# Two attention blocks on one core: zero-weight matmuls in TensorE's gaps, and first scores on 256 tokens

## The chip, the cores and the metric

The kernel runs on one core of a Trainium2 chip. The metric is the device time of one execution in microseconds, the median of several runs. The engines are TensorE (PE; its weight loads are listed apart as PEld), ScalarE (ACT), VectorE (DVE), GpSimd (POOL), and SyncE (SP), which only issues transfers here. Each runs its own list of instructions in order and waits on semaphores for the others.

## The reference, cut to what matters

Two attention blocks, A and B, on 2048 tokens of width 1024 with 32 heads of width 32, all in bf16. Their outputs stand side by side. A is full attention. B works on four segments of 512 tokens, with causal attention in a segment and a memory M, z of all segments before it.

```python
# A
qkv = x @ wqkv; q, k, v = heads of it
p = softmax(q k^T * 32**-0.5); a = (p v) @ wo
# B: for segment s of 4
logits = qs ks^T * scale + causal mask
a_dot = softmax(logits) @ vs
phi = lambda t: where(t > 0, t + 1, exp(t))
a_mem = (phi(qs) @ M) / (phi(qs) @ z + 1e-6)
o = g * a_mem + (1 - g) * a_dot            # g = sigmoid(beta), per head
M = M + phi(ks)^T @ vs;  z = z + sum of phi(ks)
b = o @ wo
return concatenate([a, b], -1)
```

## The kernel before

The order of instructions on each engine is made by a small event-driven scheduler in the Python program that builds the kernel. Each piece of work is a process that asks for an engine, with what it reads and writes, an assumed cost and a priority. The scheduler plays all engines with these costs and so fixes each engine's list; semaphore waits follow from what is read and written. At run time nothing is reordered.

The work comes in units. A unit of A is one group of four heads and 256 queries; it has eight batches, each of 256 keys. A batch is eight score matmuls (`s_batch`), two exponentials of 128x1024 on ScalarE (`exps`), which read PSUM and write PT, and later sixteen matmuls (`pv_unit`) that take PT times V and PT times ones, for output and denominator. Three pairs of PSUM banks hold scores; two further banks (`side`) serve all else.

```python
PAIRS = [(0, 1), (2, 3), (4, 5)]
OB, SB = 6, 7
RING = 27                                  # PT buffers of 512; slots are pairs, RING // 2
par = dict(b=(12, 7, 2), mem=4, ..., ahead=28, ..., ob=2, ..., wob=40, ...)

# s_batch: needs K of 512 tokens and Q of 512 tokens
yield ("ev", ("KA", g, k // 2))
yield ("ev", ("QA", g, u[2] // 2))
...
# exps
yield do("ACT", lambda e: e.activation(ap, self.ps[:, pr[0]:pr[1] + 1, :], ACTF.Exp, scale=sc), ...)   # L900
```

A projection (`proj`, `job`) takes 512 tokens: eight steps of four matmuls side by side, then a copy out of PSUM on VectorE.

```python
def job(self, due, mm, keys, out, okey, wkeys, ...):
    bank, = yield acq(self.side, 1, due)
    for i in range(n):
        yield do("PE", lambda e, i=i: mm(e, i, bank), ..., cost=N512, ...)                             # L610
    op = yield do(eng, lambda e: out(e, bank, eng), r=[("ps", bank)] + ..., cost=c, prio=1)            # L616, L617
```

The start loads the first four tiles of x (128 tokens each), transposes them on TensorE and copies them to xA, in turn on VectorE and ScalarE. Matmuls on zeros (`warm`) stand between. The other 1536 tokens come by transposing DMA. After a `yield do` of a transfer the process goes on when the transfer is issued, so an event such as `("XS", 2)` orders issues and is no wait for data.

```python
# first_x
banks = yield acq(self.pairs, 3)
for t in range(4):
    Q.spawn(self.load_xs(t, "SP" if t % 2 == 0 else "ACT"))          # L570
yield self.warm(8)                                                    # L532
for t in range(4):
    ...                                    # eight transpositions of 128x128, L550
    yield self.warm((4, 4, 4, 8)[t])
    if t % 2 == 0:                         # DVE tensor_copy, L557
    else:                                  # ACT copy, L559
...
Q.give(self.pairs, list(PAIRS))
# rest_x: six transposing DMAs of 256 tokens, L579
# first_w: weights of K (SP) and Q (ACT) after the four x tiles, of V later, L480
# a_prep order: K 0, Q 0, K 1, V 0, K 2, V 1, ...
```

The end of a unit copies the whole bank, output and denominator, in one piece; phi of B is computed on VectorE, since `po=(1, 1)` chooses this branch always.

```python
# finish
yield do("DVE", lambda e: e.tensor_copy(OD[:, :], self.ps[:, OB, :]), ...)                             # L1028
# b_mem: phi (L719 to L731), then the memory's matmuls (L746, L774) with
due = self.first[("B", n)] + self.par["mem"]
# b_proj: before block n, waits for ("fin", "B", n-2) and ("memB", n-2)
# out_B: eight output rows of a segment, each due par["ob"] after the one before                       # L1075
```

Of the kernel before, what the change touches and what calls it, by code (L numbers as in the profile page):

```python
# [9 lines left out]
ALU = mybir.AluOpType  # L10
# [3 lines left out]
P = 128  # L14
# [157 lines left out]
class Sched:  # L172
# [3 lines left out]
    def __init__(self, rec):  # L176
        self.R = rec
        self.now = 0.0
        self.heap = []
        self.seq = 0  # L180
        self.q = {e: [] for e in Recorder.ENG}
        self.free = {e: 0.0 for e in Recorder.ENG}
        self.wake = {e: None for e in Recorder.ENG}
        self.busy = {e: 0.0 for e in Recorder.ENG}
        self.mode = None
        self.dma_free = 0.0
        self.margin = {}
        self.hold = {}
        self.events = {}
        self.log = []  # L190
        self.nproc = 0

# [85 lines left out]
    def dispatch(self, eng, t):  # L278
        if self.wake[eng] != t:
            return  # L280
        self.wake[eng] = None
        if self.free[eng] > self.now + 1e-9:
            self.kick(eng)
            return
        best, soon = None, None
        for rq in self.q[eng]:
            ready = 0.0
            for d in self.R.deps("SP" if rq.kb else eng, rq.r, rq.w, rq.order):
                if d.eng != eng and d.end + LAT > ready:
                    lat = LAT  # L290
                    if rq.prio != 0 or eng != "PE":
                        lat += self.margin.get((eng, d.eng[0]), 0.0)
                    ready = max(ready, d.end + lat)
                elif d.eng == eng and d.end + (LAT if rq.order else 0) > ready:
                    ready = d.end + (LAT if rq.order else 0)
            p = rq.prio() if callable(rq.prio) else rq.prio
            if p > 0 and self.hold.get(eng, 0.0) > ready:
                ready = self.hold[eng]
            if ready <= self.now + 1e-9:
                if best is None or (p, rq.seq) < best[0]:  # L300
                    best = ((p, rq.seq), rq)
            elif soon is None or ready < soon:
                soon = ready
        if best is None:
            if soon is not None:
                self.wake[eng] = soon
                self.at(soon, lambda: self.dispatch(eng, soon))
            return
        rq = best[1]
        self.q[eng].remove(rq)  # L310
        assert all(k in self.R.lastw for k in rq.r), rq.r
        op = self.R.add("SP" if rq.kb else eng, rq.fn, rq.r, rq.w, rq.order, eng)
        cost = rq.cost
        if eng == "PE":
            if rq.mode != self.mode:
                cost += 0.1
                self.mode = rq.mode
        start = self.now
        self.free[eng] = start + cost
        op.end = start + cost + rq.tail  # L320
        if rq.kb:
            self.dma_free = max(self.dma_free, start + min(cost, 0.6)) + rq.kb / 230
            op.end = max(start + cost, self.dma_free) + 1.7
        self.busy[eng] += cost
        self.hold[eng] = start + cost + rq.hold if rq.hold else 0.0
        self.log.append((eng, start, cost, rq.mode))
        if rq.proc is not None:
            self.step(rq.proc, op)
        self.kick(eng)
# [31 lines left out]
RING = 27  # L361
# [4 lines left out]
class Kernel:  # L366
    par = dict(b=(12, 7, 2), mem=4, memM=2, span=50, rate=0.58, ahead=28, sl=4, pv=24, ob=2, lead=5, b0=1, bpos=16, wob=40, mg=0.05, off=0, oks=(1, 4), sh=2, pd=4, o0=4, od=8, run=6, po=(1, 1), fp=2)
# [48 lines left out]
    def alloc(self):  # L416
# [39 lines left out]
        self.ones32 = sb("ones32", [P, 32])  # L456
        self.maskbd = sb("maskbd", [P, P], F32)
# [53 lines left out]
    def constants(self):  # L511
# [5 lines left out]
        yield pool(lambda e: e.memset(self.ones32[:, :], 1.0), ["ones32"])  # L517
        for i in range(2):
            yield pool(lambda e, i=i: e.memset(self.VB[i][:, :, :], 1.0), [("VB", i)])
# [15 lines left out]

    def first_x(self):
        Q = self.Q
        banks = yield acq(self.pairs, 3)
        banks = [b for pr in banks for b in pr]
        for t in range(4):  # L540
            Q.spawn(self.load_xs(t, "SP" if t % 2 == 0 else "ACT"))
        yield do("DVE", lambda e: e.memset(self.PT[:, 0, :], 0.0), w=[("PT", 0)], cost=0.3, prio=0)
        yield self.warm(8)
        for t in range(4):
            yield ("ev", ("XS", t))
            b = banks[t]

            def f(e, t=t, b=b):
                for i in range(NI):
                    ins = e.transpose(self.psb[:, b, P * i:P * i + P], self.XS[:, t, P * i:P * i + P], self.ident[:, :])  # L550
                return ins
            yield do("PE", f, r=[("XS", t), "ident"], w=[("ps", b)], cost=0.9, prio=0, mode=FULL)
            yield self.warm((4, 4, 4, 8)[t])
            src = self.psb[:, b, :].rearrange("p (i n) -> p i n", i=NI)
            dst = self.xA[:, :, P * t:P * t + P]
            if t % 2 == 0:
                Q.spawn(self.one(do("DVE", lambda e, s=src, d=dst: e.tensor_copy(d, s), r=[("ps", b)], w=[("xA", 0, t)], cost=0.6, prio=0), t))  # L557
            else:
                Q.spawn(self.one(do("ACT", lambda e, s=src, d=dst: e.copy(d, s), r=[("ps", b)], w=[("xA", 0, t)], cost=1.0, prio=0), t))  # L559
        for t in range(4):  # L560
            yield ("ev", ("x0t", t))
        Q.fire(("xA", 0))
        Q.give(self.pairs, list(PAIRS))
# [9 lines left out]
    def rest_x(self):  # L573
        yield ("ev", ("WA", 1, 0))
# [9 lines left out]
    def job(self, due, mm, keys, out, okey, wkeys, scale=None, eng="DVE", cost=None, okeys=(), gate=None):  # L584
# [3 lines left out]
        n = len(keys)  # L588
        for i in range(n):
            if gate and gate[0] == i:  # L590
                yield ("ev", gate[1])
            yield do("PE", lambda e, i=i: mm(e, i, bank), r=keys[i] + list(wkeys), w=[("ps", bank)], cost=N512,
                     prio=(lambda: self.jprio(due)) if i == 0 else (lambda: min(self.jprio(due), self.par["run"])), mode=COL)
        if eng == "any":
            eng = "ACT" if (self.s_done and Q.free["ACT"] < Q.free["DVE"]) else "DVE"
        c = dve(512) if eng == "DVE" else 0.6
# [10 lines left out]
    def proj(self, due, W, wkey, x, xkeys, dst, dkey, scale=None):  # L607
        def mm(e, i, bank):
            for c in range(4):
                ins = e.matmul(self.ps[32 * c:32 * c + 32, bank, :], W[:, i, 32 * c:32 * c + 32], x(i),  # L610
# [3 lines left out]
        def out(e, bank, eng):  # L614
            if scale is None:
                return e.tensor_copy(dst, self.ps[:, bank, :])  # L616
            return e.tensor_scalar(dst, self.ps[:, bank, :], scale, None, ALU.mult)  # L617
        return (yield from self.job(due, mm, [xkeys] * NI, out, [dkey], [wkey]))
# [5 lines left out]
    def a_prep(self, g):  # L624
# [6 lines left out]
        xk = lambda c: [("xA", c, t) for t in range(4)]  # L631
        x = lambda c: (lambda i: self.xA[:, i, 512 * c:512 * c + 512])
# [8 lines left out]
        order += [("Q", 1), ("Q", 2), ("Q", 3)]  # L641
        kind = {"K": 0, "Q": 1, "V": 2}
        for w, c in order:
            k = kind[w]
            yield ("ev", ("WA", k, g))
            yield ("ev", ("xA", c))
# [3 lines left out]
            cs = slice(512 * c, 512 * c + 512)  # L650
            if w == "V":
                vt = c % 2
                op = yield from self.proj(d, self.WA[k], ("WA", k), x(c), xk(c), self.VT[vt][:, :], ("VT", vt))
                Q.spawn(self.v_turn(b, c, vt, g))
            else:
                dst = (self.KA if w == "K" else self.QA)[b]
                op = yield from self.proj(d, self.WA[k], ("WA", k), x(c), xk(c), dst[:, cs], (w + "A", b, c),
                                          QSC if w == "Q" else None)
                Q.fire((w + "A", g, c))
# [18 lines left out]
    def b_proj(self, n):  # L678
# [8 lines left out]
        for k in range(3):  # L687
# [5 lines left out]
            if k < 2:  # L693
                yield from self.proj(d, self.WB[k], ("WB", k), x, ["xB"], KQ[:, k, :], ("KQB", b, k))
            else:
                yield from self.proj(d, self.WB[k], ("WB", k), x, ["xB"], self.VT[n % 2][:, :], ("VT", n % 2))
# [124 lines left out]
    def s_all(self):  # L821
# [3 lines left out]
        self.s_done = True  # L825
        Q.fire("s_done")
# [5 lines left out]
    def s_batch(self, u, k):  # L832
# [3 lines left out]
        if u[0] == "A":  # L836
            g = u[1]
            b = g % 2
            yield ("ev", ("KA", g, k // 2))
            yield ("ev", ("QA", g, u[2] // 2))  # L840
# [3 lines left out]
            keys = [("KA", b, k // 2), ("QA", b, u[2] // 2)]  # L844
# [115 lines left out]
    def pv_unit(self, u, steps, half):  # L960
# [14 lines left out]
        for si, (k, parts) in enumerate(steps):  # L975
# [9 lines left out]
            for pi, (t, o, w, off) in enumerate(parts):  # L985
# [23 lines left out]
                first = False  # L1009
            if u[0] == "A" or half == 1 or False:  # L1010
# [294 lines left out]
    def main(self):  # L1305
# [15 lines left out]
        self.ods = Pool(range(2))  # L1321
        self.slots = Pool([((0, 2 * i), (0, 2 * i + 1)) for i in range(RING // 2)])
# [21 lines left out]
        def first_w():  # L1344
            yield ("ev", ("XS", 2))
            yield ("ev", ("XS", 3))
            Q.spawn(self.load_WA(0, 0, 0, "SP"))
            Q.spawn(self.load_WA(1, 0, 0, "ACT"))
            yield ("ev", ("xA", 1))
# [71 lines left out]
```

## Time and profile before

| | before |
|---|---|
| median of 3 runs | 1140.68 us (1138.59 to 1142.12) |
| span of the profiled execution | 1136.9 us |
| mean granted TensorE clock | 0.991 |
| busy: PE, DVE, ACT, POOL | 1046.7, 722.3, 1093.7, 140.8 us |

How to read the profile: for each engine it has the busy time; for each line the group of instructions, with its number, its busy time, the mean length of one, and the engine's idle time just before them with what ended it. A timeline row has the start, the length, the engine, line, operation, what is written and read, how many, and in brackets the idle time before. The granted clock is the share of full speed that TensorE was given. Ends of matmuls are modelled, so a busy TensorE is not one at its peak.

### The profile page before, as it was taken

To read this page: it belongs to the slowest core of one execution; us is meant where nothing else is said; L and a number is where in the kernel's file an instruction comes from. 1 tells how busy PE (TensorE), PEld (TensorE's weight loads), DVE (VectorE), ACT (ScalarE), POOL (GpSimd) and SP (SyncE) were. 2 spreads that over 40 slices of the span, in tenths; PEclk is the share of its full clock that TensorE was granted. 3 is DMA by queue.
4 is the path that set the end of the run, shared out by engine and by line. 5 is a ranking of instruction groups with operands and counts; after the bars stand their busy time and mean duration, and the time that the engine had idled before them with its cause. 6 is when DMAs were issued, how large, how long until landed. Compare 5 with 4: busy or idle time off the path is not lost.

```text
span 1136.9 us, 49940 instructions
## 1 busy us (share of the span) xinstructions
PE 1046.7 (92%) x23164; PEld 504.8 (44%) x23165; DVE 722.3 (64%) x1459; ACT 1093.7 (96%) x1192; POOL 140.8 (12%) x285
## 2 busy tenths in 40 slices
PE   8988999998899999989999999899999999989997
PEld 3434444444344444444444444344444444444444
DVE  1337556645785687788975877878676775763333
ACT  5979999999999999999999999999998999999995
POOL 1002102001111111111110210302111111110000
PEclk9989999999999999999999999999999999999999
DMA  9425332233111222225211223233113124100111
GB/s 181 100 44 125 66 63 50 58 58 76 40 49 31 54 58 59 44 44 105 53 48 37 53 54 59 48 80 56 39 46 70 31 45 122 36 26 33 38 40 52
DMA packets 214841, 67.28 MB, mean 59 GB/s; under 512 B 203872, under 2 KB 212064, under 8 KB 214624
## 3 DMA queue, kind: packets, MB, share of 16 engines
q1 hardware_dynamic: 213296, 63.20, 26.3%
q8 instruction: 184, 3.01, 1.1%
q10 hardware_dynamic: 1328, 0.79, 0.3%
q14 instruction: 33, 0.27, 0.1%
HBM read 36.70 MB, written 8.39 MB: 40 GB/s over the span
## 4 chain that ended last, share of the span: by engine, by line
ACT 85%; PE 8%; DVE 3%; SPq 2%; issue 1%; DMA 1%; POOL 0%; ACTq 0%
ACT PT L900 85%; PE ps L610 3%; PE ps L1005 3%; PE ps L1075 2%; PE ps L873 1%; SPq L579 1%; DMA OTA<-in_A_x_dram 0%; POOL PT L909 0%; DVE we L935 0%; DVE we L936 0%; DVE OD L1028 0%; ACT OTA L900 0%; DVE VT L616 0%; DMA VA<-VT 0%; DVE ze L934 0%
## 5 line engine op out<-in xcount | busy, mean ns | idle before, releaser
L900 ACT ACTIVATE PT<-ps 128x1024 bf16<-128x1024 f32 x1168 | 1073.3, 1183 | 16.6 <-PE ps L873 16.5
L1005 PE MATMUL ps<-PT,ones 128*32 128x256 bf16 (+1 forms) x4800 | 294.2, 271 | 0.0
L1005 PE MATMUL ps<-PT,VA 128*32 128x256 bf16 x4032 | 251.8, 276 | 16.6 <-ACT PT L900 13.3
L873 PE MATMUL ps<-QA,KA 32*128 32x256 bf16 x4096 | 204.6, 274 | 40.0 <-ACT PT L900 28.2
L909 POOL TENSOR_SCALAR_AFFINE_SELECT PT<-PT 128x256 bf16<-128x256 bf16 (+1 forms) x224 | 109.0, 494 | 821.6 <-ACT PT L900 816.4
L610 PE MATMUL ps<-xA,WA 128*32 128x512 bf16 x3072 | 209.5, 386 | 1.3 <-DVE KQB L616 0.3
L610 PE MATMUL ps<-xB,WB 128*32 128x512 bf16 x3072 | 203.6, 381 | 2.5 <-DVE OD L1028 0.9
L873 PEld LDWEIGHTS ps<-QA,KA 32*128 32x128 bf16 x4096 | 60.8, 92 | 218.2 <-ACT PT L900 203.7
L1005 PEld LDWEIGHTS ps<-PT,VA 128*32 128x32 bf16 x4032 | 107.6, 96 | 84.2 <-ACT PT L900 31.3
L1005 PEld LDWEIGHTS ps<-PT,ones 128*32 128x32 bf16 x4800 | 129.2, 97 | 25.6 <-issue 2.1
L610 PEld LDWEIGHTS ps<-xA,WA 128*32 128x32 bf16 x3072 | 72.9, 97 | 75.8 <-issue 28.7
L610 PEld LDWEIGHTS ps<-xB,WB 128*32 128x32 bf16 x3072 | 72.8, 96 | 73.1 <-issue 28.0
L1081 DVE CAST outsb<-ps 128x512 bf16<-128x512 f32 x60 | 41.4, 689 | 97.3 <-PE ps L1075 97.3
L1028 DVE COPY OD<-ps 128x512 f32<-128x512 f32 x128 | 87.3, 682 | 23.5 <-PE ps L1005 22.9
L616 DVE CAST VT<-ps 128x512 bf16<-128x512 f32 x64 | 44.0, 687 | 89.9 <-PE ps L610 86.4
L616 DVE CAST KQB<-ps 128x512 bf16<-128x512 f32 x64 | 44.0, 688 | 59.5 <-PE ps L610 59.3
L1075 PE MATMUL ps<-WoB,OTB 128*32 128x512 bf16 x1024 | 67.7, 381 | 0.4
L1075 PE MATMUL ps<-xA,OTA 128*32 128x512 bf16 x1024 | 65.6, 381 | 0.0
L1005 PE MATMUL ps<-PT,VB 128*32 128x256 bf16 (+1 forms) x768 | 46.8, 263 | 14.1 <-DVE OD L1028 5.7
L1034 DVE STREAM_TRANSPOSE OD<-Rall 128x256 f32<-128x256 f32 x128 | 56.6, 442 | 3.6
L1031 DVE STREAM_TRANSPOSE Dt<-OD 128x256 f32<-128x256 f32 x128 | 55.6, 435 | 2.5
L873 PE MATMUL ps<-KQB 32*128 32x128 bf16 (+3 forms) x512 | 43.4, 302 | 6.3 <-ACT PT L900 4.2
(75 smaller groups left out, 639.9 us busy)
## 6 DMA issues: line engine op xcount, KB each, us to landing
WB<-in_B_wk_dram SPq DMA_DIRECT2D x32, 256.0 KB, 3.0
WB<-in_B_wq_dram SPq DMA_DIRECT2D x32, 256.0 KB, 2.9
WB<-in_B_wv_dram SPq DMA_DIRECT2D x32, 256.0 KB, 3.4
out_dram<-outsb SPq DMA_DIRECT2D x64, 128.0 KB, 1.8
WA<-in_A_wqkv_dram SPq DMA_DIRECT2D x23, 256.0 KB, 3.1
WoB<-in_B_wo_dram SPq DMA_DIRECT2D x1, 2048.0 KB, 9.8
xA<-in_A_wo_dram SPq DMA_DIRECT2D x1, 2048.0 KB, 9.6
OTA<-in_A_x_dram ACTq DMA_DIRECT2D x2, 256.0 KB, 4.2
```

Source lines behind the costliest of these rows:

```text
L579: yield do("SP", lambda e, q0=q0, src=src: e.dma_start(self.xA[:, :, q0:q0 + 2 * P], src, transpose=True), r=[("XS", 3), ("XS", 2), ("XS", ...
L610: ins = e.matmul(self.ps[32 * c:32 * c + 32, bank, :], W[:, i, 32 * c:32 * c + 32], x(i), start=(i == 0), stop=(i == NI - 1))
L616: return e.tensor_copy(dst, self.ps[:, bank, :])
L873: ins = e.matmul(self.ps[:, bk, col:col + w], lhs(t, hs), rhs(q0, w, hs), start=True, stop=True)
L900: yield do("ACT", lambda e: e.activation(ap, self.ps[:, pr[0]:pr[1] + 1, :], ACTF.Exp, scale=sc), r=[("ps", bk) for bk in pr], w=keys, cos ...
L909: yield do("POOL", lambda e, m=m, n=n: e.affine_select(m, m, pattern=[[0, n], [1, P]], compare_op=ALU.is_ge, fill=0.0, base=0, channel_mul ...
L1005: ins = e.matmul(out, l, r, start=st, stop=sp)
L1028: yield do("DVE", lambda e: e.tensor_copy(OD[:, :], self.ps[:, OB, :]), r=[("ps", OB)], w=[("OD", x), ("Rb", x)], cost=dve(2 * QU), prio=0 ...
L1031: yield do("DVE", lambda e: e.transpose(Dt[:, :], Rb), r=[("Rb", x)], w=[("Dt", x)], cost=dve(QU), prio=self.par["fp"], hold=0.15)
L1034: yield do("DVE", lambda e: e.transpose(Rb.rearrange("p (a b) -> p a b", b=32), self.spread(Rc)), r=[("Rc", ui % 64)], w=[("Rb", x)], cost ...
L1075: ins = e.matmul(self.ps[32 * c:32 * c + 32, bank, :], lhs(j)[:, 32 * c:32 * c + 32], W(j), start=(j == 0), stop=(j == NG - 1))
L1081: return f(self.outsb[ob][:, :], self.ps[:, bank, :])
```

## The change

It has five parts. (1) The schedule can put in zero-weight matmuls: where TensorE would find nothing ready for at least 0.15 us, and its assumed load in the last 3.4 us is at most 65%, and one of the two side banks is in mid-accumulation, four matmuls of 32 zero weights on 256 columns are added to that bank. They add zero to the sum; their purpose is to keep TensorE's activity up. They end with the last scores. (2) First scores on 256 tokens: the first K and Q of group 0 are projected in two halves, and a batch waits for the half it reads. (3) The start's order: x tiles 0 and 1, then weights of K and Q, then x tiles 2 and 3; twelve warming matmuls in place of 28; all four copies to xA on VectorE; banks given back in parts. (4) RING 28 in place of 27, so 14 pairs of slots in place of 13. (5) Due times: the memory's matmuls six places earlier, output rows of B one place apart and not two, WoB's load at place 60 and not 40. (`oks` has no effect with `off=0`.)

The copy of a bank in one piece and phi on VectorE are in both versions.

```diff
-RING = 27
+RING = 28
-    par = dict(b=(12, 7, 2), mem=4, ..., ob=2, ..., wob=40, ..., oks=(1, 4), ...)
+    par = dict(b=(12, 7, 2), mem=-2, ..., ob=1, ..., wob=60, ..., oks=(0, 3), ..., fil=0.65, fs=0.15)
+        self.zero = sb("zero", [P, 32])
 # scheduler, no work ready on this engine
         if best is None:
+            if eng == "PE" and self.fill:
+                rq = self.fill(soon)
 ...
+    def filler(self, soon):
+        if self.s_done or not self.pos or not self.par["fil"] or (soon is not None and soon < now + self.par["fs"]):
+            return None
+        while Q.recent and Q.recent[0][0] < now - 3.4:
+            Q.recent.pop(0)
+        if sum(c for _, c in Q.recent) > self.par["fil"] * 3.4:
+            return None
 ...
+        zero, src = self.zero[:, :], self.maskbd.bitcast(BF)[:, 0:256]
+            for c in range(4):
+                ins = e.matmul(self.ps[32 * c:32 * c + 32, bank, 0:256], zero, src, start=False, stop=False)
 # first_x
-            yield self.warm((4, 4, 4, 8)[t])
+            if t == 1:
+                yield self.warm(4)
+                Q.give(self.pairs, [pairs[2]])
-            if t % 2 == 0:
-                Q.spawn(self.one(do("DVE", lambda e, s=src, d=dst: e.tensor_copy(d, s), ...
-            else:
-                Q.spawn(self.one(do("ACT", lambda e, s=src, d=dst: e.copy(d, s), ...
+            Q.spawn(self.one(do("DVE", lambda e, s=src, d=dst: e.tensor_copy(d, s), ...
 # a_prep
+        if g == 0:
+            todo[0:2] = [("K", 0, 0, 2), ("Q", 0, 0, 2), ("K", 0, 2, 4), ("Q", 0, 2, 4)]
 # s_batch
-            yield ("ev", ("KA", g, k // 2))
-            yield ("ev", ("QA", g, u[2] // 2))
+            yield ("ev", ("KA", g, k))
+            yield ("ev", ("QA", g, u[2]))
 # first_w
-            yield ("ev", ("XS", 2))
-            yield ("ev", ("XS", 3))
+            Q.spawn(self.load_xs(0, "SP"))
+            Q.spawn(self.load_xs(1, "ACT"))
+            yield ("ev", ("XS", 0))
+            yield ("ev", ("XS", 1))
             Q.spawn(self.load_WA(0, 0, 0, "SP"))
             Q.spawn(self.load_WA(1, 0, 0, "ACT"))
+            yield ("ev", ("WA", 0, 0))
+            yield ("ev", ("WA", 1, 0))
+            Q.spawn(self.load_xs(2, "SP"))
+            Q.spawn(self.load_xs(3, "ACT"))
```

## The prediction

> **What bounds the kernel now.** I read the engine table first, then the chain of waits, then the waits of ScalarE, then the timeline of both ends, and last the windows of a few microseconds in which ScalarE was not full.
>
> ```profile
> PE 1046.7 (92%) x23164; PEld 504.8 (44%) x23165; DVE 722.3 (64%) x1459; ACT 1093.7 (96%) x1192; POOL 140.8 (12%) x285
> ...
> ACT 85%; PE 8%; DVE 3%; SPq 2%; issue 1%; DMA 1%; POOL 0%; ACTq 0%
> ...
> L900 ACT ACTIVATE PT<-ps 128x1024 bf16<-128x1024 f32 x1168 | 1073.3, 1183 | 16.6 <-PE ps L873 16.5
> ```
>
> ScalarE (ACT) is busy 1093.7 of 1136.9 us, and the last chain runs through it for 85% of the span. Its work is one instruction, the exponential at line 900: 1168 of them, 1073.3 us, so 0.919 us each in sequence (the 1183 ns are the length of one, and neighbours overlap). Sixteen more go to borrowed tiles (WoB and OTA), 7.44 in the first eight and 7.6 in the others, so 1088.3 us in all. The change touches neither their number nor their shape. It can only win what ScalarE does not spend on exponentials: 1136.9 - 1093.7 = 43.2 us of idle time, and two copies of 1.01 us each before the first exponential. I split the 43.2 us by the timeline of ScalarE.
>
> ```profile
> 2.18 1.28 ACT L559 ACT_TABLE_LOAD   x1 [2.18 <-issue]
> 6.86 1.01 ACT L559 COPY xA<-ps 128x1024 bf16<-128x1024 bf16 x1 [3.40 <-PE ps L550]
> 9.48 1.01 ACT L559 COPY xA<-ps 128x1024 bf16<-128x1024 bf16 x1 [1.61 <-PE ps L550]
> 15.99 7.44 ACT L900 ACTIVATE WoB<-ps 128x1024 bf16<-128x1024 f32 x8 [5.49 <-PE ps L873]
> ...
> 64.38 1.94 ACT L900 ACTIVATE PT<-ps 128x1024 bf16<-128x1024 f32 x2 [4.17 <-PE ps L873]
> ...
> 263.69 35.86 ACT L900 ACTIVATE PT<-ps 128x1024 bf16<-128x1024 f32 x39 [1.15 <-PE ps L873]
> 300.64 176.10 ACT L900 ACTIVATE PT<-ps 128x1024 bf16<-128x1024 f32 x192 [1.10 <-PE ps L873]
> ...
> 858.52 10.19 ACT L900 ACTIVATE PT<-ps 128x1024 bf16<-128x1024 f32 x11 [5.34 <-PE ps L873]
> 868.96 252.35 ACT L900 ACTIVATE PT<-ps 128x1024 bf16<-128x1024 f32 x275 [0.25 <-PE ps L873]
> ```
>
> The number in brackets is the idle time before the row. **Start:** the first exponential runs at 15.99; of that, 1.28 + 1.01 + 1.01 is work, so 12.7 us idle. **Tail:** the last one ends at 868.96 + 252.35 = 1121.3, and the span at 1136.9; four output copies of 0.59 us lie between, so 13.2 us idle. **Middle:** the rest, 43.2 - 12.7 - 13.2 = 17.3 us, nearly the 16.6 us in the row of line 900. In it are 4.17 us at 60, 1.30 + 0.59 just after, 5.34 us at 853, 1.15 at 262, 1.10 at 300, and 0.24 + 0.52 at 737; some 2.9 us are scattered. The windows tell which of these come from TensorE's clock (columns: PE, PEld, DVE, ACT and POOL busy, then the granted clock, DMA share and GB/s).
>
> ```profile
> 60.00:64.00 4.00, 0.05 (x1) 0.06 (x1) 0.00 (x0) 0.21 (x1) 0.00 (x0) 0.79 0.34 70
> 64.00:68.00 4.00, 4.00 (x41) 1.18 (x45) 0.00 (x0) 2.33 (x3) 0.00 (x0) 0.50 0.01 4
> 260.00:264.00 4.00, 4.00 (x44) 1.21 (x46) 3.08 (x6) 2.85 (x4) 3.35 (x6) 0.57 1.03 200
> 296.00:300.00 4.00, 2.81 (x64) 1.45 (x60) 3.31 (x7) 3.54 (x4) 2.54 (x6) 0.73 0.14 28
> ```
>
> At 60 TensorE starts nothing for 3.98 us, which the chain calls "issue": all its operands were there. Then it runs at clock 0.50 until about 68.5. At 260, 298 and 735 the clock falls too, without such a gap. All other windows of 4 us up to 1124 have a clock of 1.00, but for those on either side of these places. So the clock costs ScalarE about 1.9 us after the gap at 60 and 1.15 + 1.10 + 0.76 = 3.0 us at the three other places, no more.
>
> [...] the tiles of x, from two queues, landed 3.9 to 4.9 us after issue, and the weights queued behind them only after 5.1 to 6.8 us. So what is asked for first matters.
>
> **The change, part by part.** [...]
>
> *Start.* Before: x tiles land from 4.9, four transpositions of eight instructions with 4, 4, 4 and 8 warming matmuls between and after them, projections of K and Q on 512 tokens from 11.10 to 14.7, the cast of Q 14.79 to 15.48, scores at 15.54, exponential at 15.99. After: tiles 0 and 1 and the first weights of K and Q are asked for first.
> - Transpositions of tiles 0 and 1: about 0.65 us each from 4.9, so to 6.2; four warming matmuls of 0.22, to 7.1. Sixteen of 28 warming matmuls go, 16 x 0.21 = 3.4 us, and two transpositions move behind, 1.3 us.
> - Copies to xA on VectorE, 0.69 each, done at about 7.0. The weights took 5.1 to 6.8 us from an issue at 1.7; issued at 1.2 they are there at 6.3 to 7.5.
> - K on 256 tokens: eight groups of four matmuls. The trace starts a 256-column group every 0.107 us, so 0.86 us, and as much for Q: from about 7.4 to 9.2. The cast of 256 columns, scaled from 0.69, about 0.4: 9.6. Scores and first exponential, 0.45 later as now: about **10.1**.
> - Only one batch can run on these halves: two exponentials, 1.85 us, to 12.0. The next needs the second half of K: transpositions of tiles 2 and 3 behind the first scores (9.3 to 10.8), two copies to 11.6, K to 12.6, cast and scores to 13.6. That is a gap of about 1.6 us.
>
> Gain 15.99 - 10.1 - 1.6 = **4.3 us**. It must not be given back by K of later tokens: their six transposing DMAs take 17.7 us of queue time behind the last x tile. Before, the third block of K was ready 5 us ahead of its use (cast at 25.30, needed after 16 exponentials at 31). Five microseconds less and 2 us of later DMA make this tight but should not stop ScalarE long. I take off 0.5: **-3.8**.
>
> *Zero-weight matmuls.* They are put in only where the program's own schedule sees TensorE idle and under 65% load in the last 3.4 us, and only into a bank in mid-accumulation, so they add zero and need no copy. TensorE is not busy for 1136.9 - 1046.7 = 90.2 us; at 0.107 us a group, a third of it holds about 280 groups, 30 us, beside the exponentials. Gain: most of the 3.0 us, say -2.5; nothing of the gap at 60. Cost: a group between two score groups changes the tiling of the array, and the trace shows 0.21 us of idle at each such change; some ten placed badly cost about +1.
>
> *Schedule.* RING 28 gives 14 pairs of slots where 27 // 2 gave 13; one exponential pair more of slack, -0.5. The memory update is due six places earlier. The wait of 5.34 us at 853 ends at the late projections of K and Q of a block of B, and this projection waits for the memory of two blocks before; the earlier due date may remove it. But output rows of B are also asked for at twice the rate (one place apart), and these filled TensorE just before, from 837 to 847. I count -1.3. WoB loaded later: 0, since it took 9.8 us and was not waited for.
>
> Tail: no part acts there; zero-weight matmuls stop with the last scores. 0.
>
> Sum: -3.8 - 2.5 + 1 - 0.5 - 1.3 = **-7.1**, so 1140.7 - 7.1 = 1133.6; I say **1133.5 us**.
>
> **Rivals.** (1) *The start is hidden anyway*: the DMA of x and PE work, not the first scores, set the pace to 70 us. For it: TensorE is busy 29.13 of 32 us from 28 to 60 and the chain has much of lines 610 and 1005 there. Against: ScalarE is then busy 31.18 of 32. It would leave 1138. (2) *Zero-weight matmuls in the way of scores*: TensorE is 92% busy and real score groups take longer than the schedule thinks. For: ScalarE waits for nothing but line 873. Against: three pairs of banks let scores run ahead, and the load limit. It would make about 1145. (3) *A better order in the middle*: the 5.34 and the 4.17 both vanish, since both hang on where instructions fall. It would make about 1126. (4) *The same in reverse*: a new late projection of 5 us; 1139.
>
> **Range and chances.** Between rivals 3 and 4 lies most of it: **1125 to 1141**. Two per cent is 22.8 us; faster by that needs more than half of all 43.2 us of idle time, with the start and tail still there: 0.03. Slower by that needs a new stall on a large scale: 0.02. Within: 0.95.
>
> **What would show it.** The first exponential at 10 to 11, then a hole of 1 to 2 us after two of them; no COPY on ScalarE; busy time of line 900, borrowed tiles included, within 3 us of 1088; clock 1.00 in the windows where it fell, save after a gap of issue; a new group of PE with zero weights, some 1100 instructions; the last exponential to the end still 15 to 16 us. The prediction is wrong if the idle time of line 900 rises above 20 us, if the tail moves by over 3 us, or if the first exponential is not before 12.

## The result, and the profile after

The changed kernel took 1134.85 us, median of 4 runs (1133.5 to 1135.25), beside 1140.79 us for the kernel before. The ratio is 0.9948, with a 95% interval of 0.993 to 0.9966: 5.9 us, half a per cent, faster. The forecast was 1133.5 us in a range of 1125 to 1141. The sum held. Its terms did not, as the experiments show.

First the page of the changed kernel: the engine table, the chain by engine, and the exponentials (now line 953).

```profile
PE 1052.7 (93%) x23589; PEld 514.0 (45%) x23589; DVE 720.3 (64%) x1463; ACT 1091.9 (96%) x1190; POOL 132.8 (12%) x286
...
ACT 82%; PE 11%; DVE 3%; DMA 1%; issue 1%; POOL 0%; DVEq 0%
...
L953 ACT ACTIVATE PT<-ps 128x1024 bf16<-128x1024 f32 x1168 | 1073.0, 1183 | 14.6 <-PE ps L926 14.5
```

ScalarE has two instructions less, the copies to xA. Its exponentials cost what they did, 1073.0 for 1073.3 us. It is still the bound. What changed is where it waits, so the timeline of ScalarE in the changed kernel is the view to read.

```profile
10.99 1.94 ACT L953 ACTIVATE WoB<-ps 128x1024 bf16<-128x1024 f32 x2 [7.35 <-PE ps L926]
13.59 1.94 ACT L953 ACTIVATE WoB<-ps 128x1024 bf16<-128x1024 f32 x2 [0.66 <-PE ps L926]
...
42.55 1.94 ACT L953 ACTIVATE PT<-ps 128x1024 bf16<-128x1024 f32 x2 [1.56 <-PE ps L926]
47.14 7.44 ACT L953 ACTIVATE PT<-ps 128x1024 bf16<-128x1024 f32 x8 [2.65 <-PE ps L926]
...
62.11 0.21 ACT L517 ACTIVATE gcol<-beta 128x8 f32<-128x8 bf16 x1 [1.49 <-DMA beta<-in_B_beta_dram]
64.86 1.94 ACT L953 ACTIVATE PT<-ps 128x1024 bf16<-128x1024 f32 x2 [2.54 <-PE ps L926]
68.38 123.00 ACT L953 ACTIVATE PT<-ps 128x1024 bf16<-128x1024 f32 x134 [1.58 <-PE ps L926]
...
892.73 224.69 ACT L953 ACTIVATE PT<-ps 128x1024 bf16<-128x1024 f32 x245 [0.91 <-PE ps L926]
```

In the kernel before, these are the rows at the fiftieth exponential:

```profile
67.61 1.94 ACT L900 ACTIVATE PT<-ps 128x1024 bf16<-128x1024 f32 x2 [1.30 <-PE ps L873]
70.14 28.72 ACT L900 ACTIVATE PT<-ps 128x1024 bf16<-128x1024 f32 x31 [0.59 <-PE ps L873]
```

The first exponential runs at 10.99 for 15.99 before: five microseconds of lead. Then count exponentials. Before, the fiftieth ends at 69.5 us (67.61 + 1.94). Here it is the second of those that begin at 68.38, and it ends at 70.3. **The lead of the start is gone, and 0.8 us more.** From there to the last exponential it is 1121.3 - 69.5 = 1051.8 us before, and 892.73 + 224.69 - 70.3 = 1047.1 after: 4.7 us gained. The wait of 5.34 us before 858.52 has no counterpart, and the small waits together are 0.8 us longer: from the fiftieth exponential to the last ScalarE idles 5.7 us ahead of exponentials where it idled 10.2. The tail is 15.4 for 15.6 us. So in the two profiled executions the net of 4.1 us arose in the middle. The medians are 5.9 us apart; the profiled execution of the kernel before was the shortest of its four (1138.59 us), so some 2 us of the gain lie outside these two traces.

The windows of 4 us in which the clock fell, in the changed kernel (PE, PEld, DVE, ACT, POOL busy, clock, DMA share, GB/s):

```profile
64.00:68.00 4.00, 3.92 (x63) 1.96 (x63) 0.69 (x1) 1.94 (x2) 0.00 (x0) 0.62 0.02 4
...
264.00:268.00 4.00, 2.84 (x80) 1.95 (x76) 3.01 (x10) 4.00 (x5) 0.22 (x1) 0.79 0.49 104
268.00:272.00 4.00, 4.00 (x78) 1.72 (x72) 0.76 (x2) 2.55 (x4) 0.00 (x0) 0.79 0.00 0
```

With 68 to 72 (0.96) these are all up to the tail. The drops near 298 and 735 are gone; the one near 260 has moved to 266, and ScalarE waited 1.45 us for it. The zero-weight matmuls are few. The row of the tile `zero` in the trace gives their count, the shortest, median and longest duration of one in ns, and when they ran:

```profile
L570 PE MATMUL ps<-maskbd,zero x376: 271/273/421, 40.4 to 980.4; 128*32 128x256 bf16 x188
```

376 / 4 is 94 groups in the whole run, on the way from 40 to 980 us.

### The profile page after: what moved, and what is told of

It reads as the page before. It is cut to its first block, busy times and chain, and to the rows that moved or that the text cites. A ratio compares the mean times of both kernels' runs of the same rounds, so it can differ in the third digit from the quotient of the medians.

```text
span 1132.8 us, 50803 instructions
## 1 busy us (share of the span) xinstructions
PE 1052.7 (93%) x23589; PEld 514.0 (45%) x23589; DVE 720.3 (64%) x1463; ACT 1091.9 (96%) x1190; POOL 132.8 (12%) x286
## 4 chain that ended last, share of the span: by engine, by line
ACT 82%; PE 11%; DVE 3%; DMA 1%; issue 1%; POOL 0%; DVEq 0%
ACT PT L953 81%; PE ps L653 4%; PE ps L1058 3%; PE ps L1132 2%; PE ps L926 2%; DMA VA<-VT 1%; DMA PKt<-PH 1%; DVE OD L1085 0%; ACT OTA L953 0%; PE ps L546 0%; DVE VT L659 0%; DVE we L988 0%; POOL PT L962 0%; ACT WoB L953 0%; DVE we L989 0%
## 5 line engine op out<-in xcount | busy, mean ns | idle before, releaser
L953 ACT ACTIVATE PT<-ps 128x1024 bf16<-128x1024 f32 x1168 | 1073.0, 1183 | 14.6 <-PE ps L926 14.5
L653 PE MATMUL ps<-xA,WA 128*32 128x512 bf16 (+1 forms) x3136 | 204.3, 378 | 8.5 <-issue 4.6
L962 POOL TENSOR_SCALAR_AFFINE_SELECT PT<-PT 128x256 bf16<-128x256 bf16 (+1 forms) x224 | 104.0, 470 | 821.1 <-ACT PT L953 815.8
```

The source lines that it names most:

```text
L653: ins = e.matmul(self.ps[32 * c:32 * c + 32, bank, 0:n], W[:, i, 32 * c:32 * c + 32], x(i), start=(i == 0), stop=(i == NI - 1))
L962: yield do("POOL", lambda e, m=m, n=n: e.affine_select(m, m, pattern=[[0, n], [1, P]], compare_op=ALU.is_ge, fill=0.0, base=0, channel_mul ...
```

## The experiments

Each run gives its ratio to the kernel before on the same chip, with the 95% interval. The changed kernel stands at 0.9948 (0.993 to 0.9966). All runs compute the full output.

### One part at a time, on the kernel before

**The new start alone** (order of loads, 12 warming matmuls, copies on VectorE, halves of K and Q; all else as before).

```diff
 # the changed kernel with
-RING = 28;  mem=-2, ob=1, wob=60, fil=0.65
+RING = 27;  mem=4, ob=2, wob=40, no zero-weight matmuls
```

> The kernel before with the new start alone (order of loads, 12 warming matmuls, copies on VectorE, first K and Q by halves). My forecast's sum had -3.8 us for it. Rival, after the two traces: the first exponential comes 5 us earlier, but the lead is used up before 70 us, because the transposing DMAs of x start 2 us later and the fourth block of V is no earlier; then the time is that of before within 1 us, with the 5.34 us wait at 853 still there.

Measured: **1.0001** (0.9991 to 1.0012). My -3.8 us falls; the rival holds. The first exponential is at 11.07, and the timeline of ScalarE in this run shows where the lead went:

```profile
11.07 1.94 ACT L953 ACTIVATE WoB<-ps 128x1024 bf16<-128x1024 f32 x2 [7.42 <-PE ps L926]
...
42.02 3.77 ACT L953 ACTIVATE PT<-ps 128x1024 bf16<-128x1024 f32 x4 [3.19 <-PE ps L926]
```

The wait of 3.19 us comes after 2 + 2 + 4 + 8 + 12 = 28 exponentials. At the start there are 29 pairs of slots, 13 of the ring and 16 borrowed, and a batch takes two, so 28 fit. In the changed kernel, with 14 of the ring, 30 fit, and the waits come after 30 and 32. So scores wait for slots, and slots come free when PT times V has been done. The timeline of all engines in the changed kernel shows what that waits for:

```profile
41.31 1.20 SPq L665 DMA_TRANSPOSE VA<-VT  x1
...
45.70 0.29 PE L1058 MATMUL ps<-PT,VA 128*32 128x256 bf16 x4 [1.14 <-DMA VA<-VT]
...
46.69 0.40 PE L926 MATMUL ps<-QA,KA 32*128 32x256 bf16 x8
47.14 7.44 ACT L953 ACTIVATE PT<-ps 128x1024 bf16<-128x1024 f32 x8 [2.65 <-PE ps L926]
```

The fourth block of V is turned (transposed) by a DMA issued at 41.31. The kernel before issues the same DMA at 41.61:

```profile
41.61 1.20 SPq L622 DMA_TRANSPOSE VA<-VT  x1
```

The exponentials began five microseconds sooner, V did not. Over all traces a little of the lead may be left: the fiftieth exponential ends at 67.9 to 70.3 us in the six with the new start (x_first, below, left out) and at 69.5 to 71.9 in the seven with the old one, the means one microsecond apart.

**The zero-weight matmuls alone.**

```diff
 # the kernel before with
+fil=0.65, fs=0.15, self.Q.fill = self.filler
```

> The kernel before with the zero-weight matmuls alone. Theory: the stretches of half clock at 260, 298 and 735 us go, -2.5 to -3 us, and the waits of 4.2 us at 60 and 5.3 us at 853 stay. Rival: the groups land beside work that was not late, the time is that of before within 1 us. If they got in the way of scores it would be +1 us or more.

Measured: **0.9998** (0.9987 to 1.0009): nothing. 64 groups were put in (256 matmuls). The drops at 260 and 735 went, the one at 298 stayed (0.75 and 0.82 from 296 to 304), and others came, at 28 to 32 (0.57) and 212 to 216 (0.59).

**The memory's due time alone.**

```diff
-    par = dict(..., mem=4, ...)
+    par = dict(..., mem=-2, ...)
```

> The kernel before with the memory's matmuls due six places earlier, alone. Theory: this removes the wait of 5.34 us at 853, so -4 to -5 us. Rival: that wait comes from the output rows of B or from the order at large, then it stays and the time is that of before within 1 us.

Measured: **0.9972** (0.9962 to 0.9981), or -3.2 us, short of the -4 to -5 expected: in its profile the wait near 853 shrinks from 5.34 to 2.75 us and does not go. This is the only part that wins by itself.

**The fourteenth pair of slots alone.**

```diff
-RING = 27
+RING = 28
```

> The kernel before with 14 pairs of slots in place of 13, alone. Theory: 0 to -0.5 us, since the exponentials wait for scores and not for slots. Rival: the late projections at 853 come from the order at large, so that any change of order removes the wait of 5.34 us; then -4 to -5 us here too.

Measured: **1.0038** (1.0024 to 1.0053), or +4.3 us, outside both expectations. The wait near 855 is still there with 5.20 us; new ones are one of 2.26 at 770 and one of 1.32 at 737, the former with the clock at 0.54 and 0.60 from 768 to 776.

**The due times of output rows and of WoB's load alone.**

```diff
-    par = dict(..., ob=2, ..., wob=40, ...)
+    par = dict(..., ob=1, ..., wob=60, ...)
```

> The kernel before with the due times of the output rows of B (one place apart) and of WoB's load (place 60) alone. Theory: the rows of a segment are over sooner, so the projections of the next block of B come a little sooner and the wait of 5.34 us at 853 shrinks: -1 to -3 us. Rival: the earlier rows push the projections further back: +1 to +3 us.

Measured: **1.0024** (1.0012 to 1.0036), or +2.7 us: the rival. The wait stays with 5.05, and 1.48 and 0.80 us come just ahead of it. The two due times moved together here, so the run does not tell which of them costs.

The product of the five is 1.0001 x 0.9998 x 0.9972 x 1.0038 x 1.0024 = 1.0033, and the whole change is 0.9948. **The parts do not add.** So I took parts out of the whole.

### One part left out of the changed kernel

```diff
 # full_no_fill
-        self.Q.fill = self.filler
 # full_mem_4
-mem=-2
+mem=4
 # full_ring_27
-RING = 28
+RING = 27
```

> The changed kernel without the zero-weight matmuls; the order is free to differ after the first place where one stood. Theory: they are worth nothing by themselves, the time is that of the changed kernel within 1.5 us, and the clock falls in more windows than with them. Rival: with the other parts they are needed, +3 us or more.

> The changed kernel with the memory's matmuls due where they were. Theory: the gain is theirs, so +3.5 to +6 us, and a wait of several us for late projections of B comes back near 850. Rival: with the new due times of the rows it does not come back, and the time moves by less than 1.5 us.

> The changed kernel with 13 pairs of slots. By itself the fourteenth pair made the kernel before 4.4 us slower. If a pair more is harmful as such, this is faster by 3 to 5 us; if its effect is that of one order among many, it can go either way, within 3 us.

And with the start of the kernel before:

```diff
 # full_old_start: first_x, rest_x and first_w as before, K and Q of group 0 not halved
-            todo[0:2] = [("K", 0, 0, 2), ("Q", 0, 0, 2), ("K", 0, 2, 4), ("Q", 0, 2, 4)]
```

> The changed kernel with the old start. By itself the new start moved the kernel before by nothing. If its lead is lost by 70 us here as well, this is within 1 us of the changed kernel. If the other parts let it keep the lead, it is 3 to 4 us slower.

| left out | ratio to before | 95% interval |
|---|---|---|
| nothing | 0.9948 | 0.993 to 0.9966 |
| zero-weight matmuls | 0.9955 | 0.9938 to 0.9971 |
| memory six places earlier | 0.9940 | 0.9923 to 0.9956 |
| new start | 0.9956 | 0.9943 to 0.9969 |
| fourteenth pair | 0.9994 | 0.9982 to 1.0006 |

Without zero-weight matmuls, or with the old start, the time is that of the changed kernel within the intervals. Both are worth nothing that these runs can show, alone or with the rest. Without the zero-weight matmuls the clock falls in more windows: one minus the granted share, summed over time up to the tail, is 10.2 us, for 3.4 us with them and 8.5 us in the kernel before. That is one trace of each kernel. Over the profiled executions of all 14 programs the mean granted clock is 0.993 to 0.996 in the seven with zero-weight matmuls and 0.985 to 0.995 in the seven without. So the clock fell less with them on the whole, and a change of order alone moves it as much. ScalarE does not show it. The memory's due time, the one part that wins alone, is not missed in the whole: my theory for that run fell. The pair of slots, harmful alone, is needed in the whole.

### What the gain hangs on

Parts that mean nothing for scores act through the order of instructions that the scheduler makes. So I looked for what ends the wait near 853 in the order itself. From the timeline of the kernel before:

```profile
847.06 0.69 DVE L1081 CAST outsb<-ps 128x512 bf16<-128x512 f32 x1 [0.87 <-PE ps L1075]
847.67 0.41 DVE L1060 TENSOR_TENSOR OTB<-tB,amem 128x256 bf16<-128x256 f32 x1
...
851.48 1.90 PE L610 MATMUL ps<-xB,WB 128*32 128x512 bf16 x32
...
857.33 0.69 DVE L616 CAST KQB<-ps 128x512 bf16<-128x512 f32 x1 [0.46 <-PE ps L610]
858.08 0.39 PE L873 MATMUL ps<-KQB 32*128 32x512 bf16 x4 [0.15 <-DVE KQB L616]
```

At 847.06 the eighth output row of the third segment leaves PSUM. Only then may block 24 of B, the first of the fourth segment, write the second half of its result to OTB, at 847.67, since these rows read OTB. With that block 24 is finished, and only then does the scheduler let block 26, which uses the buffers of block 24, project K and Q. Q is there at 858, and all scores wait behind those of block 26. This last step is a rule of the Python program (`b_proj` waits for `("fin", "B", n-2)`) and no need of the buffers of K and Q: in the trace block 24's score matmuls read them for the last time at 802.40, 45 us before the row. A narrower rule might take the wait away without moving a row; no run tried it. In the changed kernel the same four steps, from the timeline of VectorE, and the scores of block 26 are:

```profile
834.53 0.69 DVE L1138 CAST outsb<-ps 128x512 bf16<-128x512 f32 x1 [2.35 <-PE ps L1132]
835.14 0.41 DVE L1117 TENSOR_TENSOR OTB<-tB,amem 128x256 bf16<-128x256 f32 x1
...
839.80 0.69 DVE L659 CAST KQB<-ps 128x512 bf16<-128x512 f32 x1 [0.42 <-PE ps L653]
...
843.80 0.69 DVE L659 CAST KQB<-ps 128x512 bf16<-128x512 f32 x1 [0.53 <-PE ps L653]
...
853.39 0.39 PE L926 MATMUL ps<-KQB 32*128 32x512 bf16 x4
```

The eighth row is out 12.5 us sooner and Q is ready 13.5 us sooner, at 843.80; the scores of block 26 come at 853.39 and wait for nothing. So compare the eighth row with the first scores of block 25, the block between; the time by which the row is later is called the lag here:

| run | eighth row | scores of block 25 | lag, us | wait before block 26, us |
|---|---|---|---|---|
| rows_only | 849.5 | 830.6 | 18.9 | 5.05 |
| fill_only | 851.7 | 834.4 | 17.3 | 6.40 |
| before | 847.1 | 833.1 | 14.0 | 5.34 |
| start_only | 849.4 | 835.5 | 13.9 | 5.34 |
| ring_only | 850.3 | 836.4 | 13.9 | 5.20 |
| full_ring_27 | 846.0 | 833.2 | 12.8 | 5.19 |
| mem_only | 840.3 | 832.3 | 8.0 | 2.75 |
| changed kernel | 834.5 | 834.4 | 0.1 | none |
| full_no_fill, full_old_start | 832.1, 836.7 | 832.0, 836.6 | 0.1 | none |
| x_first (below) | 834.4 | 834.2 | 0.1 | none |
| full_mem_4 | 830.6 | 834.0 | -3.4 | none |

The times go with it: the runs without the wait stand at 0.9931 to 0.9956, mem_only at 0.9972, those with all of it at 0.9994 to 1.0038. A late row costs only where the next blocks follow closely. In the kernel before, the eighth row of the second segment leaves at 603.84, 14.7 us after the first scores of block 17, and no wait follows: the scores of block 18 come 34.0 us after those of block 17, those of block 26 only 25.0 us after those of block 25, with the wait in it.

Two runs then moved the rows on purpose, by one number each.

**Rows sooner, in the kernel before.**

```diff
-    par = dict(..., od=8, ...)
+    par = dict(..., od=-20, ...)
```

> The kernel before with one number changed: the eight output rows of a segment of B are due 28 places sooner (od -20 in place of 8), so they are not held back behind other work. Theory: the wait of 5.34 us at 853 hangs on the eighth output row of the segment (in the runs so far the wait is 5 us where that row is copied out 13 to 19 us after the scores of block 25 begin, 2.75 us where it is 8 us, and none where it is 0 or less). With sooner rows that row comes 10 us or more earlier and the wait goes: -4 to -5 us. Rival: the wait comes from the memory's matmuls or from the order at large; then it stays, and rows in the way of projections make it slower by 1 to 4 us.

Measured: **1.0151** (1.0135 to 1.0168), 17 us slower. The wait went: the eighth row left at 838.5, 16.3 us ahead of the scores of block 25, and block 26 waited for nothing:

```profile
838.55 0.69 DVE L1138 CAST outsb<-ps 128x512 bf16<-128x512 f32 x1 [0.78 <-PE ps L1132]
...
854.86 0.39 PE L926 MATMUL ps<-KQB 32*128 32x512 bf16 x4
```

But the rows now stand ahead of scores in TensorE's list, and the waits of ScalarE doubled:

```profile
ACT PT L953 <- PE ps L926: 33.6, 39, 3.5
```

That is 33.6 us in 39 waits, for 16.5 us in 14 before; 15.0 us of them lie at 317 to 346, 545 to 586 and 805 to 835, where rows of the first, second and third segment are computed. Of the theory the going of the wait came true, of the rival the cost, at over four times its upper figure. The run shows that the wait follows the row, and not that this is the way to remove it.

**Rows later, in the changed kernel.**

```diff
-    par = dict(..., od=8, ...)
+    par = dict(..., od=16, ...)
```

> The changed kernel with one number changed: the eight output rows of a segment of B are due eight places, some 15 us, later (od 16 in place of 8). Nothing is put ahead of scores by it. Theory: the changed kernel gained by having the eighth row of the third segment out before the scores of block 25 begin; with later rows that row comes 8 to 15 us late again, and a wait of 3 to 5 us for projections returns near 855: +3 to +6 us against the changed kernel. Rival: the wait hung on something else in the order; then none returns near 855 and the time is within 1.5 us of the changed kernel.

Measured: **0.9984** (0.9974 to 0.9994), 4.1 us slower than the changed kernel. From its timeline:

```profile
849.26 0.69 DVE L1138 CAST outsb<-ps 128x512 bf16<-128x512 f32 x1 [2.72 <-PE ps L1132]
849.87 0.75 DVE L1117 TENSOR_TENSOR OTB<-tB,amem 128x256 bf16<-128x256 f32 x2
854.79 1.90 PE L653 MATMUL ps<-xB,WB 128*32 128x512 bf16 x32
...
859.98 0.69 DVE L659 CAST KQB<-ps 128x512 bf16<-128x512 f32 x1 [2.17 <-PE ps L653]
860.73 0.40 PE L926 MATMUL ps<-KQB 32*128 32x512 bf16 x4 [0.59 <-DVE KQB L659]
...
861.17 5.61 ACT L953 ACTIVATE PT<-ps 128x1024 bf16<-128x1024 f32 x6 [6.88 <-PE ps L926]
```

The same steps are back: row at 849.26 (lag 15.1 us), OTB, projections, scores, and ScalarE idle for 6.88 us. From the fiftieth exponential on it idles 12.6 us ahead of exponentials, 6.9 more than in the changed kernel, and this one wait is all of the difference. So the gain is, for 4.1 of its 5.9 us, and within the intervals perhaps for all, the eighth row of the third segment in time for block 26.

What stays open is why the rows begin sooner in the changed kernel. They begin when block 23 is finished, and that ends with its memory matmul: at 792.4 before and 781.1 after. The due time moved it alone from 792.4 to 787.9; yet full_mem_4 has it at 774.1 with the old due time, and full_ring_27 at 791.2 with the new one. It comes out of the order as a whole, and I did not find one cause.

### Can the start keep its lead?

The new order of loads delays the other tiles of x: their transposing DMAs begin at 8.28 us for 6.23 before. This run asks for all four x tiles ahead of the weights.

```diff
             yield ("ev", ("XS", 1))
+            Q.spawn(self.load_xs(2, "SP"))
+            Q.spawn(self.load_xs(3, "ACT"))
+            yield ("ev", ("XS", 2))
+            yield ("ev", ("XS", 3))
             Q.spawn(self.load_WA(0, 0, 0, "SP"))
             Q.spawn(self.load_WA(1, 0, 0, "ACT"))
-            yield ("ev", ("WA", 0, 0))
-            yield ("ev", ("WA", 1, 0))
-            Q.spawn(self.load_xs(2, "SP"))
-            Q.spawn(self.load_xs(3, "ACT"))
```

> The changed kernel with all four x tiles asked for ahead of the weights of K and Q, as before; all else is kept. Theory: the lead of the start was lost since the transposing DMAs of x begin 2 us later (8.28 for 6.23), so the fourth block of V is no earlier than before and the scores wait for slots at 41 and 44 us. Here they begin at about 6.3, the first exponential is half a microsecond later, and the waits at 41 and 44 shrink by up to 2 us: -1 to -2 us in time. Rival: the blocks of K and V are paced by one projection after another, 3.5 us each, and not by DMA; then these waits stay and the time is that of the changed kernel, or 0.5 us more.

Measured: **0.9931** (0.9919 to 0.9943), 1131.96 us, the lowest median of all. The DMAs begin at 6.13, the first exponential is at 11.52, and the fiftieth ends at 68.1 us, 2.2 us sooner than in the changed kernel. As the theory had it, the waits of 1.56 and 2.65 us for slots shrink, to one of 1.76. But the fourth block of V is turned at 40.64, only 0.7 us sooner for DMAs of x that begin 2.1 us sooner, so these alone do not set its pace; and the waits after the fiftieth exponential are 7.3 us for 5.7; the profiled execution, of 1135.19 us, was the longest of the six. The interval overlaps that of the changed kernel, so I do not call it faster than that; it beats the kernel before by 0.57 to 0.81%.

## Why the prediction was right, and where it was wrong

The bound, the idle time to be won and the size of the whole were right: ScalarE's exponentials did not move, two per cent was out of reach, and 5.9 us of a forecast 7.1 came. The terms of the sum were wrong in four places and cancelled, so the right number is luck: the five single runs multiply to +3.8 us, for a sum of -7.1.

- **The start.** The step "Gain 15.99 - 10.1 - 1.6 = **4.3 us**" was close on its own ground: the first exponential came at 10.99, and the holes after it were 0.66, 0.59 and twice 0.36 us, so the seventeenth began at 28.04 for 31.45, 3.4 us ahead. The step that failed is the next one, "this tight but should not stop ScalarE long. I take off 0.5". It watched K, which was in time. It left out V and the slots: after 30 exponentials there were none free. What to take off was all of it within the interval (1.0001 for the start alone). Rival 1, "The start is hidden anyway", was right, though it named DMA and TensorE's load and not the slots.
- **Zero-weight matmuls.** The term "Gain: most of the 3.0 us, say -2.5", less 1 for bad places, was 0 alone (0.9987 to 1.0009). That such matmuls would keep the clock full was my estimate; the trace of the kernel before did not show it. There are 94 groups and not 280; the clock falls less with them on the whole; and its drops cost ScalarE too little, and move too freely, for a difference to be seen. For the cost, "0.21 us of idle at each such change" is misread: 0.21 us is the least distance of starts across a change in the kernel before, for 0.11 to 0.12 between most groups of one kind, so I estimate some 0.1 us for a change, the difference of the two.
- **The pair of slots.** The term "-0.5" was +4.3 us alone. In the whole it is needed. Slack for one more batch shows only at the start (30 exponentials for 28 before the first wait for slots), where it won nothing; what moved the time was another order of everything: without the pair the wait before block 26 is back with 5.19 us.
- **The wait at 853.** Of "I count -1.3" the mechanism was half right, late projections of a block of B that wait for the second block before it. What they wait for was the row and not the memory, and I gave it a quarter of its worth: the wait of 5.34 us went whole. This is rival 3 in part: 5.34 us vanished, the stop at 60 us did not.

One reading of the clock was loose as well. After the stop at 60 it was halved from 62.3 to 69.1 us, as the shares of 0.79 from 60 to 64 and 0.86 from 68 to 72 give, so for 6.8 us and not from the end of the stop to 68.5 only, and it fell 2.3 us into the gap of 3.98.

Two signs that the forecast asked for, clock 1.00 outside the stop and about 1100 zero-weight matmuls, did not come (0.79 from 264 to 272; 376). The hole after two exponentials came with 0.66 us, below the 1 to 2 forecast. No copies on ScalarE, exponentials unchanged, a first exponential between 10 and 11 and a tail of 15 to 16 us did come.

## What to carry to other kernels

An earlier start is worth only what the first full buffer lets through: count how many steps of the bound engine fit in the slots, and look what frees the first of them. When a scheduler makes the order, a part's worth alone says little of its worth in the whole (here one part changed its sign), so test the whole with one part out, and look for the single dependency that the order decides. A long wait of the bound engine is followed back step by step, through buffers that are reused, to the last thing that was late; moving that thing on purpose in both directions shows whether it is the cause.

## What the runs showed of the hardware that I had not expected

TensorE stopped early, after nearly the same number of its own matmuls, in each of the eight programs listed here. In the changed kernel's timeline of TensorE, and in that of full_ring_27:

```profile
64.08 0.40 PE L653 MATMUL ps<-xA,WA 128*32 128x512 bf16 x3 [4.01 <-issue]
```

```profile
59.69 1.04 PE L653 MATMUL ps<-xB,WB 128*32 128x512 bf16 x15 [2.08 <-issue]
```

The matmuls recorded ahead of the stop are 985 in both. They are 986 in the kernel before, in rows_sooner and in full_old_start, 985 in full_mem_4 and rows_later and 987 in x_first, whatever the instructions were (scores, projections, PT times V) and whether the stop began at 57.6 us (full_ring_27) or at 61.35 us (rows_sooner). It lasts 3.98 us in the kernel before and 4.01 us in the changed one, 3.44 to 4.14 us in the other four of these with a long stop, 2.08 in full_ring_27 and 1.91 in x_first. Half clock began at 62.30 us in the kernel before, within the stop, and at 64.92 us in the changed kernel, 0.8 us after its end. What makes TensorE stop there was not shown. ScalarE waited 4.17 us at it in the kernel before, and in the changed kernel 1.49 + 2.54 us, with the short activation of gcol between.

The clock also halved where TensorE did not stop. In the clock records of both kernels of the change, each stretch of half clock between 20 us and the tail lasts 3.41 us, but for the one from 62.3 us in the kernel before, which lasts 6.83. TensorE was recorded busy, in the 3.41 us ahead of each, for:

| kernel | half clock from, us | busy in the 3.41 us before, us | longest gap in them, us |
|---|---|---|---|
| before | 62.30 (the stop) | 1.08 | 2.3 of the stop's 3.98 |
| before | 260.27 | 2.06 | 0.52 |
| before | 297.82 | 1.85 | 0.90 |
| before | 734.73 | 1.90 | 0.66 |
| changed | 64.92 (the stop) | 0.84 | 2.6 of the stop's 4.01 |
| changed | 266.31 | 1.79 | 0.60 |

Recorded busy time alone does not tell when the clock falls: 1.81 us from 44.44 to 47.85 in the changed kernel and 1.92 us from 509.45 to 512.86 in the kernel before, less than the 2.06 ahead of 260.27, were followed by full clock. The change's own limit, 65% of 3.4 us, is 2.2 us by the scheduler's assumed costs.
